# A short convolution and a SiLU feed-forward block: the output multiplication by 20 products over thirds and halves in place of 21, with nine sums made by DMAs that add

## Chip, cores and metric

The kernel runs on one core of one Trainium2 chip. The metric is the time of one execution on the device in microseconds; 2334.24 us is the median of three runs (2333.86 to 2334.28).

## What is computed

```python
# x (8, 4096, 192), weight (8, 7); w_in (192, 2048), w_out (2048, 192), all float32
w = softmax(weight, axis=-1)                       # one filter of 7 taps for each head of 24 channels
x_pad = concat([zeros((8, 6, 192)), x], axis=1)    # causal
out[b, s, h, g] = sum_k w[h, k] * x_pad[b, s + k, h, g]
x = out.reshape(32768, 192)
h = x @ w_in                                       # (32768, 2048)
g = h * (1 / (1 + exp(-h)))                        # SiLU
y = g @ w_out                                      # (32768, 192)
```

The weights arrive as float64 words and are rounded to float32 by integer operations at the start.

## The kernel before, in words

The 32768 tokens are worked in 32 blocks of 1024 (`TT`), each of two halves of 512 (`TB`). Block 0 is multiplied plainly (`up_plain`, `down_plain`) while the weights are still being prepared; blocks 1 to 31 use fast schemes that trade multiplications for additions.

Channels are worked in three thirds of 64 (`R`), and the 2048 hidden channels in 16 chunks of 128, in four groups of four (`NJ` = 4, index `j` or `g`).

**Up.** A block's hidden values `h` are made by 20 products (`PRODUCT`, `product`, L656) for each of the four groups. One product is a matmul with 64 rows of weights (half of TensorE's rows) that moves 512 columns, so two of them can run side by side. Their sums are finished by a list of small steps (`MICRO`, `micro`): copies and additions between PSUM banks (`b0` to `b6`), and into the tile `g`. `S13` to `S20` are the SiLUs on ScalarE, which leave eight slices `h0` to `h7` for each group in SBUF: four chunks of hidden channels, two token halves. Additions (`'a'`) are on VectorE; copies (`'c'`) are on ScalarE unless `ON_DVE` names them.

**Down, before.** `out_slot` (L746) works tiles of 32 output channels: six accumulators `acc0` to `acc5`, each fed for every group `j` and chunk `e` by four matmuls with 128 rows, 32 columns of weights and 512 moving columns, the four side by side in the columns of TensorE. For `acc5` the four move 128 columns each. Four of the operands are differences of slices of `g`, made by `sum_g` (L711), four for each group, each 128 partitions by 1024 elements, into a rotating tile `t`. The six accumulators are joined into `cmb` by `merge` (copies on ScalarE at L803, L808, L811; seven additions on VectorE at L823), turned by `turn_out` (L835) and stored by `store_out` (L845).

**Work beside it.** The next block's tokens are loaded (`load`, L289, on SP's queue), turned (`turn_in`, L548), convolved (`conv`: first tap on ScalarE at L579, six on VectorE at L582, for each third), spread over partitions by eleven SBUF to SBUF DMAs on SP's queue (`spread`, L599), and combined by six additions (`win`, L607). GpSimd does little after the start: one small copy a block (`halo_in`, L569).

**Order.** Every engine runs its instructions in program order, and that order is written out by hand: `START` for the first three blocks and `PLAN` for the steady state, strings of tokens such as `P7.0` (product 7 of group 0), `k8.2` (step k8 of group 2), `v.26` (third 2, tap 6), `sp.3`, `w.0`, `st.1`. A `+` marks the next block, a `-` the block before. So the next block's products follow the last output products of this one without a pause being written between them. PSUM has eight banks of 128 by 512, handed from step to step in the order in which they are freed (`at`, `TOUCHES`). `finish` is an ending of its own for the last block.

Of the kernel before, what the change touches and what calls it, by code (L numbers as in the profile page):

```python
# [9 lines left out]
F32 = mybir.dt.float32  # L10
I32 = mybir.dt.int32
# [6 lines left out]
def kernel(  # L18
# [40 lines left out]
    tpool = ctx.enter_context(tc.tile_pool(name="tp", bufs=3))  # L59
    gpool = ctx.enter_context(tc.tile_pool(name="gp", bufs=2 * NJ))  # L60
    upool = ctx.enter_context(tc.tile_pool(name="up", bufs=10))
# [28 lines left out]
    )  # L90
    START = (
# [1031 lines left out]
```

## Time and profile before

| | us |
|---|---|
| median of three runs | 2334.24 |
| the profiled execution, its own time | 2334.11 |
| its span, first to last instruction | 2332.4 |
| first fast product (L656) begins | 106.22 |
| one block in the steady state | 71.56 |
| last matmul ends | 2324.70 |

Mean granted TensorE clock 0.999. The busy shares are averages over the span; what a block costs is read from the chain of waits in order of time, which repeats itself with the block, and what each engine has left from the busy time in one block's window. Groups' busy times overlap each other on TensorE, where two or four matmuls run side by side, so its groups do not add up to the span. Every fp32 matmul shows as two records.

### The profile page before, as it was taken

To read this page: it belongs to the slowest core of one execution; us is meant where nothing else is said; L and a number is where in the kernel's file an instruction comes from. 1 tells how busy PE (TensorE), PEld (TensorE's weight loads), DVE (VectorE), ACT (ScalarE), POOL (GpSimd) and SP (SyncE) were. 2 spreads that over 40 slices of the span, in tenths; PEclk is the share of its full clock that TensorE was granted. 3 is DMA by queue.
4 is the path that set the end of the run, shared out by engine and by line. 5 is a ranking of instruction groups with operands and counts; after the bars stand their busy time and mean duration, and the time that the engine had idled before them with its cause. 6 is when DMAs were issued, how large, how long until landed. Compare 5 with 4: busy or idle time off the path is not lost.

```text
span 2332.4 us, 43764 instructions
## 1 busy us (share of the span) xinstructions
PE 2324.2 (100%) x17382; PEld 921.5 (40%) x17382; DVE 2178.5 (93%) x3045; ACT 1330.8 (57%) x2523; POOL 53.7 (2%) x84
## 2 busy tenths in 40 slices
PE   9999999999999999999999999999999999999998
PEld 5344343334333344333344333443334433334433
DVE  8999999999999999999999999999999999999996
ACT  5356655566654576545666555665457654566654
POOL 4200000000000000000000000000000000000000
PEclk9999999999999999999999999999999999999999
DMA  7211221212212222212122122221221221212211
GB/s 159 57 37 26 53 53 30 50 32 49 53 37 43 44 37 53 45 37 50 28 53 53 30 49 35 46 53 39 40 51 30 53 49 34 50 28 53 53 33 22
DMA packets 451246, 106.55 MB, mean 46 GB/s; under 512 B 423585, under 2 KB 428705, under 8 KB 451041
## 3 DMA queue, kind: packets, MB, share of 16 engines
q1 hardware_dynamic: 447392, 101.78, 23.3%
q8 instruction: 136, 2.23, 0.4%
q0 software_dynamic: 448, 1.58, 0.3%
q10 hardware_dynamic: 3200, 0.39, 0.1%
q14 instruction: 70, 0.57, 0.1%
HBM read 31.46 MB, written 25.17 MB: 24 GB/s over the span
## 4 chain that ended last, share of the span: by engine, by line
PE 95%; DVE 1%; SPq 0%; DMA 0%; issue 0%; ACT 0%; ACTq 0%
PE ps L746 48%; PE ps L656 47%; SPq L599 0%; DVE t L711 0%; DMA nat<-in_x_dram 0%; DVE win L607 0%; DVE u L678 0%; DVE w_other L257 0%; SPq L289 0%; DVE w_own L257 0%; DVE cmb L257 0%; DVE ps L694 0%; ACT u L257 0%; DVE g L694 0%; DVE wx L257 0%
## 5 line engine op out<-in xcount | busy, mean ns | idle before, releaser
L656 PE MATMUL ps<-win,w_own 64*128 64x512 f32 x1488 | 661.4, 598 | 0.8 <-DVE win L607 0.5
L746 PE MATMUL ps<-g,wo 128*32 128x512 f32 x2976 | 661.5, 592 | 0.0
L746 PE MATMUL ps<-t,wo 128*32 128x512 f32 (+1 forms) x4528 | 511.3, 447 | 0.0
L656 PE MATMUL ps<-dup,w_own 64*128 64x512 f32 x1240 | 492.5, 594 | 0.2 <-ACT ps L689 0.2
L746 PE MATMUL ps<-t,wx 128*32 128x512 f32 x2976 | 484.7, 592 | 0.0
L691 ACT ACTIVATE g<-ps 128x512 f32<-128x512 f32 x620 | 367.1, 599 | 186.6 <-DVE g L694 113.9
L656 PE MATMUL ps<-dup,w_other 64*128 64x512 f32 x1240 | 460.0, 595 | 0.0
L656 PE MATMUL ps<-win,w_other 64*128 64x512 f32 x992 | 444.6, 595 | 0.0
L694 DVE TENSOR_TENSOR g<-g,ps 128x512 f32<-128x512 f32 x496 | 331.3, 683 | 54.4 <-PE ps L656 35.4
L582 DVE SCALAR_TENSOR_TENSOR nat<-xt,turned,nat 128x512 f32<-128x512 f32 x558 | 378.2, 746 | 3.9 <-ACT nat L579 1.6
L808 ACT COPY yx<-ps 32x512 f32<-32x512 f32 x150 | 84.3, 579 | 516.7 <-PE ps L746 514.9
L656 PEld LDWEIGHTS ps<-win,w_own 64*128 64x128 f32 x1488 | 246.6, 186 | 211.4 <-issue 120.3
L711 DVE TENSOR_TENSOR t<-g,t 128x1024 f32<-128x1024 f32 x248 | 302.5, 1220 | 16.9 <-PE ps L746 9.6
L711 DVE TENSOR_TENSOR t<-g 128x1024 f32<-128x1024 f32 x248 | 300.6, 1212 | 13.3 <-PE ps L746 13.1
L746 PEld LDWEIGHTS ps<-t,wo 128*32 128x32 f32 x4528 | 175.1, 110 | 248.4 <-issue 189.9
L694 DVE TENSOR_TENSOR ps<-u,ps 128x512 f32<-128x512 f32 x372 | 255.3, 687 | 11.8 <-ACT u L687 5.2
L656 PEld LDWEIGHTS ps<-dup,w_own 64*128 64x128 f32 x1240 | 195.5, 186 | 142.7 <-issue 77.2
L746 PE MATMUL ps<-g,wx 128*32 128x512 f32 x1488 | 245.7, 592 | 0.0
L691 ACT ACTIVATE g<-g 128x512 f32<-128x512 f32 x372 | 220.8, 625 | 27.1 <-DVE g L694 23.6
L689 ACT ACTIVATE ps<-ps 128x512 f32<-128x512 f32 x372 | 214.5, 584 | 36.0 <-DVE ps L694 19.0
L746 PEld LDWEIGHTS ps<-g,wo 128*32 128x32 f32 x2976 | 173.1, 110 | 148.0 <-issue 147.2
L656 PEld LDWEIGHTS ps<-dup,w_other 64*128 64x128 f32 x1240 | 167.8, 186 | 131.3 <-ACT ps L689 50.3
(102 smaller groups left out, 1826.3 us busy)
## 6 DMA issues: line engine op xcount, KB each, us to landing
dup<-nat SPq DMA_DIRECT2D x221, 128.0 KB, 2.3
nat<-in_x_dram SPq DMA_DIRECT2D x382, 64.0 KB, 2.4
out_dram<-t SPq DMA_DIRECT2D x372, 64.0 KB, 2.0
win<-nat SPq DMA_DIRECT2D x124, 128.0 KB, 2.4
raw<-in_moe_w_out_dram SPq DMA_DIRECT2D x8, 384.0 KB, 3.9
raw<-in_moe_w_in_dram SPq DMA_DIRECT2D x12, 192.0 KB, 5.0
w_other<-w_own POOLq DMA_DIRECT2D x8, 192.0 KB, 5.6
raw<-in_moe_w_in_dram SPq DMA_DIRECT2D x6, 128.0 KB, 3.4
```

The source lines that it names most:

```text
L582: nc.vector.scalar_tensor_tensor(out=dst, in0=src, scalar=tap, in1=dst, op0=ALU.mult, op1=ALU.add)
L656: nc.tensor.matmul(at(b, "bank", to, g), raw(g, w, e), rows(slot_of(b, x_), e), start=first, stop=True, skip_group_check=True,)
L689: pin(nc.scalar.activation(seen[to], seen[u], AF.Copy, scale=-1.0))
L691: pin(nc.scalar.activation(seen[to], seen[u], AF.Silu, scale=float(sign)))
L694: pin(nc.vector.tensor_tensor(seen[to], seen[u], seen[v], op=op))
L711: pin(nc.vector.tensor_tensor(t[i // 2][:, i % 2, :], u, v, op=ALU.subtract))
L746: nc.tensor.matmul(acc[SQ * q : SQ * q + SQ, to], lhs[:, e, SQ * k : SQ * k + SQ], rhs[:, e, ts(q, TB // 4) if i == 5 else to], start=firs ...
L808: pin(nc.scalar.copy(to, acc(3 * (name[0] == "x") + k)[n:P, :]))
```

## The change

**Down, after.** The output is now made by 20 products (`OUT`) of 4 chunks by channel thirds by token halves. Groups are taken in pairs: `q` = 0 holds groups 0 and 1, `q` = 1 groups 2 and 3. One product `Qr.q` is four matmuls: for each of the pair's two groups (`e`) and each half `h` of the slot's 512 columns, one with 128 rows, 64 columns of weights and 256 moving columns, the two halves side by side in TensorE's columns.

```diff
+    def out_slot(b, r, q):
+        w, slot, name = OUT[r]
         acc = at(b, "bank", name)
+        for e in range(2):
+            for h in range(2):
+                pin(
+                    nc.tensor.matmul(
+                        acc[R * h : R * h + R, 0:HT],
+                        wd[:, 2 * q + e, w, :],
+                        g_all[:, q, slot, e, ts(h, HT)],
+                        start=False,
+                        stop=True,
+                        skip_group_check=True,
+                    )
+                )
```

**Operands.** All slices of `h` lie in one tile, `g_all`: two pairs, eleven slots (0 to 7 are the SiLUs' results, 8 to 10 are further), 128 by 1024 each. Thirteen sums for each pair work in place in it, 26 a block; nine of them are DMAs issued by GpSimd that add the source to the destination.

```diff
-        pin(nc.vector.tensor_tensor(t[i // 2][:, i % 2, :], u, v, op=ALU.subtract))
+    def sum_g(b, name, q):
+        sign, to, u, v = SUMS[name]
+        if f"{name}.{q}" in BY_DMA:
+            pin(
+                nc.gpsimd.dma_start(
+                    out=flat(g_all[:, q, to]), in_=flat(g_all[:, q, u + v - to]), accum_op=ALU.add
+                )
+            )
+            return
+        to, u, v = (flat(g_all[:, q, s]) for s in (to, u, v))
+        pin(nc.vector.tensor_tensor(to, u, v, op=ALU.add if sign > 0 else ALU.subtract))
...
+    SUMS = {'s1': (1, 8, 5, 3),
+            's2': (1, 9, 8, 2),
+            's4': (1, 7, 7, 5),
+            's3': (1, 9, 4, 9),
+            's6': (-1, 10, 0, 9),
+            's7': (1, 8, 8, 10),
+            's8': (1, 1, 1, 10),
+            's9': (1, 7, 7, 1),
+            's10': (-1, 5, 8, 7),
+            's12': (1, 5, 2, 5),
+            's0': (1, 3, 3, 2),
+            's5': (1, 6, 6, 4),
+            's11': (1, 6, 6, 7)}
...
+    BY_DMA = ('s0.0', 's0.1', 's11.0', 's11.1', 's4.0', 's4.1', 's7.0', 's7.1', 's8.1')
```

So `s8.1` is slot 1 plus slot 10 of pair 1. `OUT[r]` names the weights, the slot read and the bank; for this text: Q0, Q19, Q6 read slot 7 (as it came, after s4, after s9), Q13 and Q9 slot 8 (before and after s7), Q8 slot 10, Q16 slot 9, Q12 and Q10 slot 5 (after s10 and s12), Q5 slot 1, Q4 slot 6 after s11.

**Joining.** In place of `merge`: steps of the kind of `MICRO` on 128 by 256, of names with D: two zero fills on ScalarE and one on VectorE (`Dz`), twelve copies (`Dk`, `Dh`, `Du`; two on VectorE, ten on ScalarE), nine additions on VectorE (`Di`, `Dj`), and six transposes (`DS`) of 128 by 256 in place of four of 96 by 512. Stores are 2 times 4 DMAs of 96 KB a block in place of 4 times 3 of 64 KB. `finish` goes: the last block ends as every block does.

**Weights of the output.** `combine_out` makes the 20 combinations by 25 operations of 128 by 4 by 64 in four parts (`co.0` to `co.3`), which now stand among the first fast block's products, in place of 16 of 128 by 192, the first four of which stood ahead of them.

**Order.** `START` and `PLAN` are written anew. In the steady state the output products stand in this order, with VectorE's and GpSimd's steps between them (`*` marks the DMAs that add; P and the up steps left out):

```
s1.0 Q11.0 s2.0 v.05 s0.0* Q0.1 s4.1* Q11.1 Q13.0 s1.1 Q13.1 Q0.0 Q2.0 Q16.0 s2.1 Q16.1 Q19.1
s4.0* v.24 s3.0 Q14.0 Q14.1 s6.0 Q2.1 s7.0* Q8.0 s3.1 Q19.0 s6.1 v.16 Q1.1 Q8.1 s8.0 v.06 Q18.1
Q3.1 Q1.0 Q3.0 Q7.0 -DS13.0 s9.0 Q7.1 s10.0 Q12.0 Q18.0 sp.6 s8.1* sp.3 Q9.0 v.25 s9.1 s7.1* Q9.1
v.26 s5.1 -st.0 sp.0 s10.1 Q12.1 s12.0 Q10.0 +i.1 s12.1 Q6.0 Q6.1 Q10.1 Di12_7.0 s0.1* Q5.1 Q17.1
Q15.1 Q15.0 s5.0 Q17.0 s11.1* sp.5 +ld.2 +ld.0 +i.0 sp.7 sp.4 sp.8 Q5.0 sp.1 +i.2 sp.10 sp.9 s11.0*
w.0 sp.2 Q4.0 w.2 w.1 w.3 w.4 Q4.1 w.5 +P7.0 ...
```

`ON_DVE` names eleven copies of 128 by 512 in place of ten, besides the D steps above. Raw weights and the rounding's scratch lie in fixed places of `g_all`, `u_all` and `fin` in place of rotating tiles.

More of the change, by code (lines that the diff above doesn't have):

```diff
@@ L246 @@
     FLIPS = (1, 1, -1)
-    ON_DVE = ('h15.3', 'h18.0', 'k12.0', 'k12.1', 'k12.3', 'k8.0', 'u10.1', 'u10.2', 'u10.3', 'u6.2')
-    CLOSING = "S14.3"
+    ON_DVE = ('Dk15.0', 'Dk5.0', 'Dz1.0', 'h17.1', 'h17.3', 'h18.0', 'h18.3', 'k12.0', 'k12.1', 'k17.1',
+              'k8.3', 'k9.3', 'u10.0', 'u6.3')
+    SUMS = {'s1': (1, 8, 5, 3),
[11 more added lines that the diff above has]
+            's11': (1, 6, 6, 7)}
+    OUT = {0: (7, 7, 'ob0'),
+           1: (12, 6, 'ob1'),
+           2: (16, 5, 'ob8'),
+           3: (11, 6, 'ob3'),
+           4: (14, 6, 'ob5'),
+           5: (15, 1, 'ob7'),
+           6: (1, 7, 'ob0'),
+           7: (19, 0, 'ob3'),
+           8: (10, 10, 'ob3'),
+           9: (2, 8, 'ob4'),
+           10: (17, 5, 'ob2'),
+           11: (9, 1, 'ob0'),
+           12: (0, 5, 'ob0'),
+           13: (13, 8, 'ob1'),
+           14: (8, 2, 'ob6'),
+           15: (5, 9, 'ob3'),
+           16: (4, 9, 'ob1'),
+           17: (18, 3, 'ob2'),
+           18: (3, 4, 'ob1'),
+           19: (6, 7, 'ob8')}
+    COMBINE_OUT = [(1, 12, 10, 9), (-1, 13, 7, 8), (1, 14, 11, 9), (-1, 15, 6, 14), (-1, 16, 5, 8),
[4 rows of a table added]
+    NEGATE_OUT = [4, 19]
+    BY_DMA = ('s0.0', 's0.1', 's11.0', 's11.1', 's4.0', 's4.1', 's7.0', 's7.1', 's8.1')
+    SLOTS = 11
     def pin(ins):
@@ L276, in at, with flat @@
         return tile_
-    nats, xts, gs = {}, {}, {}
+    nats, xts = {}, {}
+    g_all = const.tile([P, 2, SLOTS, 2, TB], F32, name="g")
+    u_all = const.tile([P, 10, TB], F32, name="u")
+    HT = TB // 2
+    fin = const.tile([P, 14, HT], F32, name="fin")
+    def flat(t):
+        names = "abcd"[: len(t.shape) - 1]
+        return t.rearrange(f"p {' '.join(names)} -> p ({' '.join(names)})")
     def load(b, ks=range(NK)):
@@ L358 @@
     wr, ws = ([t[:, j] for j in range(NJ)] for t in (w_own, w_other))
-    wo = [const.tile([P, 2, 2, D], F32, name=f"wo{j}") for j in range(NJ)]
-    wx = [const.tile([P, 3, 2, HD], F32, name=f"wx{j}") for j in range(NJ)]
+    wd = const.tile([P, NJ, 20, R], F32, name="wd")
     raws = {}
     def raw_tile(key):
-        pool, tag = (gpool, "g") if key in (("i", 2), ("i", 3)) else (tpool, "t")
-        raws[key] = pool.tile([P, 4 * TB], I32, tag=tag, name="raw")[:, 0 : 2 * WC]
+        place = {
+            ("i", 0): g_all[:, 0, 8:10],
+            ("i", 1): g_all[:, 1, 8:10],
+            ("i", 2): fin[:, 0:6],
+            ("i", 3): fin[:, 6:12],
+            ("o", 0): u_all[:, 5:8],
+            ("o", 1): g_all[:, 0, 8:10],
+            ("o", 2): g_all[:, 1, 8:10],
+            ("o", 3): fin[:, 0:6],
+        }[key]
+        raws[key] = flat(place).bitcast(I32)[:, 0 : 2 * WC]
         return raws[key]
@@ L486, in combine, with combine_out @@
                 eng.tensor_scalar(both(to), both(u), scalar1=-1.0, scalar2=None, op0=ALU.mult)
-    def combine_out(j):
-        def a_(u, a):
-            return wo[j][:, a, :, HD * u : HD * u + HD]
-        x_ = [wx[j][:, i, :, :] for i in range(3)]
-        vec.tensor_tensor(x_[0], a_(1, 0), a_(1, 1), op=ALU.add)
-        vec.tensor_tensor(x_[1], x_[0], a_(0, 0), op=ALU.subtract)
-        vec.tensor_tensor(x_[2], a_(0, 1), x_[1], op=ALU.subtract)
-        vec.tensor_tensor(a_(1, 0), a_(0, 0), a_(1, 0), op=ALU.subtract)
+    def combine_out(part):
+        work = [*COMBINE_OUT, *((0, s, s, s) for s in NEGATE_OUT)]
+        n = (len(work) + 3) // 4
+        for sign, to, u, v in work[n * part : n * part + n]:
+            to, u, v = (wd[:, :, s, :] for s in (to, u, v))
+            if sign:
+                vec.tensor_tensor(to, u, v, op=ALU.add if sign > 0 else ALU.subtract)
+            else:
+                vec.tensor_scalar(to, u, scalar1=-1.0, scalar2=None, op0=ALU.mult)
     load_in(0, nc.sync, (0,))
@@ L616, in rows, with g_slot @@
         return t[R * e : R * e + R]
-    def g_tile(b, j, a):
-        if (b, j, a) not in gs:
-            gs[b, j, a] = gs[1, j, a] if b > 1 else gpool.tile([P, 2, 2, TB], F32, tag="g", name="g")
-        return gs[b, j, a]
+    def g_slot(j, c, n):
+        return g_all[:, j // 2, 2 * c + n, j % 2, :]
     def up_plain(b, j):
@@ L670, in place @@
             if x_[0] == "h":
-                c, n = divmod(int(x_[1:]), 2)
-                return g_tile(b, g, c // 2)[:, n, c % 2, :]
+                return g_slot(g, *divmod(int(x_[1:]), 2))
+            if x_[0] == "o":
+                if x_[1] == "b":
+                    return at(b, "bank", x_)[:, 0:HT]
+                return fin[:, (6 if x_[1] == "h" else 12) + int(x_[2:])]
             return at(b, "bank" if x_[0] == "b" else "up", x_, g)
-        seen = {x_: place(x_) for x_ in dict.fromkeys((to, u, v)) if x_}
+        seen = {x_: place(x_) for x_ in dict.fromkeys((to, u, v)) if isinstance(x_, str)}
         if kind == "c" and f"{name}.{g}" in ON_DVE:
@@ L689, in micro @@
                 pin(nc.scalar.activation(seen[to], seen[u], AF.Copy, scale=-1.0))
+        elif kind == "z":
+            if f"{name}.{g}" in ON_DVE:
+                pin(nc.vector.memset(seen[to], 0.0))
+            else:
+                to_ = seen[to].rearrange("p (x c) -> p x c", x=2)
+                pin(nc.scalar.copy(to_, zeros.unsqueeze(1).to_broadcast([P, 2, P])))
+        elif kind == "t":
+            k, n = to
+            pin(nc.vector.transpose(osb_all[:, NK * n + k, :], seen[u]))
         elif kind == "s":
@@ L713, in seed @@
-    def seed(b):
-        pin(nc.vector.memset(at(b, "bank", "acc5")[:, 0 : TB // 4], 0.0))
-    def out_slot(b, j, i, e, half=None):
-        w, x_ = wo[j], wx[j]
-        name = f"acc{6 if i == 3 and half else i}"
-        first = i != 5 and (b, name) not in begun
-        begun.add((b, name))
-        acc = at(b, "bank", name)
-        ts_ = {
-            k: held_at[b, f"t{k}", j] if half == 0 else sums_of(b, j, k)
-            for k in ((), (), (0,), (1,), (0, 1), (1,))[i]
-        }
-        def t(k):
-            return ts_[k // 2][:, k % 2, :].rearrange("p (e t) -> p e t", e=2)
-        a_ = [[w[:, a, :, HD * u : HD * u + HD] for a in range(2)] for u in range(2)]
-        forms = {
-            1: lambda: (a_[0][0], gs[b, j, 0][:, 0]),
-            2: lambda: (a_[0][1], gs[b, j, 1][:, 0]),
-            3: lambda: (x_[:, 2], gs[b, j, 1][:, 1]),
-            4: lambda: (a_[1][1], t(3)),
-            5: lambda: (x_[:, 0], t(0)),
-            6: lambda: (x_[:, 1], t(1)),
-            7: lambda: (a_[1][0], t(2)),
-        }
-        own, other, c = ((1, 2, 0), (3, 2, 1), (6, 2, 2), (7, 4, 0), (5, 4, 1), (4, 4, 2))[i]
-        for q in range(4):
-            lhs, rhs = forms[own if q < NP else other]()
-            k = c if i == 5 or q == NP else q
-            to = slice(0, TB // 4) if i == 5 else slice(0, TB) if half is None else ts(half, TB // 2)
-            pin(
-                nc.tensor.matmul(
-                    acc[SQ * q : SQ * q + SQ, to],
-                    lhs[:, e, SQ * k : SQ * k + SQ],
-                    rhs[:, e, ts(q, TB // 4) if i == 5 else to],
-                    start=first,
-                    stop=True,
-                    skip_group_check=True,
-                )
-            )
@@ L773, in down_plain @@
                             )
-                        if (a, e, k) == (1, 1, NK - 1):
-                            for c in range(2):
-                                del gs[b, j, c]
                         yield
     def copy_plain(b, k):
-        pin(nc.scalar.copy(cmbs[b][0][:, k, :], at(b, "bank", f"plain{k}")))
-    def merge(b, name, q):
-        n = HD
-        def acc(i):
-            return at(b, "bank", f"acc{i}")
-        if b not in cmbs:
-            new = b == 1
-            cmb = xpool.tile([P, 4, TB], F32, tag="cmb", name="cmb") if new else cmbs[1][0]
-            cmbs[b] = [cmb, {}]
-        cmb, t = cmbs[b]
-        c = [cmb[0:n, i, :] for i in range(4)]
-        if name[0] in "xy":
-            if name[0] not in t:
-                t[name[0]] = xpool.tile([P, TB], F32, tag="yx", name="yx", bufs=2)
-            k = int(name[1])
-            to = t[name[0]][SQ * k : SQ * k + SQ, :]
-            if name == "x2":
-                pin(
-                    nc.scalar.copy(
-                        to[:, ts(q, TB // 4)], acc(5)[SQ * q : SQ * q + SQ, 0 : TB // 4]
-                    )
-                )
-            else:
-                pin(nc.scalar.copy(to, acc(3 * (name[0] == "x") + k)[n:P, :]))
@@ new lines, in copy_plain, with turn_out, store_out @@
+        pin(nc.scalar.copy(plain[:, k, :], at(b, "bank", f"plain{k}")))
+    def turn_out(b, k):
+        pin(nc.vector.transpose(flat(osb_all[:, 2 * k : 2 * k + 2, :]), plain[:, k, :]))
+    def store_out(b, i):
+        if not b:
+            osb = osb_all.rearrange("p (k x) t -> p k (x t)", k=NK).rearrange(
+                "p k (a c) -> p k a c", c=SQ
+            )
+            for q in range(P // SQ):
+                c = R * i + SQ * (q % 2)
+                pin(
+                    nc.sync.dma_start(
+                        out=out_v[2 * b + q // 2][:, :, c : c + SQ],
+                        in_=osb[SQ * q : SQ * q + SQ, i, :, :],
+                    )
+                )
@@ L823, in merge @@
-        pin(nc.vector.tensor_tensor(out_, u, v, op=ALU.add))
-    osbs = {}
-    def osb_of(b):
-        t = at(b, "t", "osb" if b else "osb0")
-        return t.rearrange("p i (k c) -> p (i k c)", c=SQ).rearrange("p (i k c) -> p i k c", i=4, c=SQ)
-    def turn_out(b, i):
-        osb = osb_of(b)
-        top = HD if b else P
-        pin(
-            nc.vector.transpose(
-                osb[0:top, i, :, :].rearrange("p k c -> p (k c)"), cmbs[b][0][0:top, i, :]
-            )
-        )
-    def store_out(b, i):
-        osb = osb_of(b)
-        for q in range((HD if b else P) // SQ):
-            n, c = (i % 2, HD * (i // 2) + SQ * q) if b else (q // 2, R * i + SQ * (q % 2))
-            pin(
-                nc.sync.dma_start(
-                    out=out_v[2 * b + n][:, :, c : c + SQ],
-                    in_=osb[SQ * q : SQ * q + SQ, i, :, :],
-                )
-            )
+        osb = osb_all[:, NK * i : NK * i + NK, :].rearrange("p m (k c) -> p m k c", c=SQ)
@@ L851 @@
+        nk = HT // SQ
+        for r in range(P // SQ):
+            to = out_v[2 * b + i][:, nk * (r // 2) : nk * (r // 2) + nk, :]
+            to = to.rearrange("t k (m s c) -> t m k s c", m=NK, c=SQ)[:, :, :, r % 2, :]
+            pin(nc.sync.dma_start(out=to, in_=osb[SQ * r : SQ * r + SQ]))
     plan = [slot.split() for slot in (PLAN,)]
-    did, later = set(), []
+    did = set()
     BACK = {"-": 1, "=": 2, "+": -1}
     base = {t.lstrip("-=+") for s in plan for t in s}
-    held = {
-        t
-        for t in base
-        if t.split(".")[0] not in MICRO
-        and (t[0] in "Mzyxo" and t[:2] != "ze" or t[:2] == "st" or t[0] in "Dt" and int(t.split(".")[1][0]) >= NJ // 2)
-    }
@@ L867, in step @@
         if b < 0 or b >= NB or not name or (b, token) in did:
-            return
-        if b == NB - 1 and token in held:
-            return
-        if b == NB - 1 and token[:3] == "D3." and (b, CLOSING) not in did:
-            later.append(token)
             return
@@ L879, in step @@
             product(b, int(name[1:]), *digits)
-        elif name == "ze":
-            seed(b)
-        elif name == "t":
-            sum_g(b, *digits)
-        elif name[0] == "D":
-            i, (j, e) = int(name[1]), digits
-            for half in range(2) if i == 3 and b == NB - 1 else (None,):
-                out_slot(b, j, i, e, half)
-        elif name[0] in "Mzyx":
-            merge(b, name, *digits)
+        elif name[0] == "Q":
+            out_slot(b, int(name[1:]), *digits)
+        elif name in SUMS:
+            sum_g(b, name, *digits)
         elif name == "o":
@@ L1081 @@
     homes["bank"].extend(bank() for _ in range(8))
-    homes["up"].extend(upool.tile([P, TB], F32, tag="u", name="u") for _ in range(10))
-    homes["t"].extend(tpool.tile([P, 2, 2 * TB], F32, tag="t", name="t") for _ in range(3))
+    homes["up"].extend(u_all[:, i, :] for i in range(10))
     downs = down_plain(0)
```

180 lines of the change are left out of this document (53 added, 127 removed), and 186 rows, old and new, of tables (COMBINE_OUT, PLAN, START).

## The prediction, made before the changed kernel ran

> **What bounds the kernel now.** I read the page's first part, then the chain of waits, then one block of that chain in order of time, then what VectorE has left in that block.
>
> ```profile
> PE 2324.2 (100%) x17382; PEld 921.5 (40%) x17382; DVE 2178.5 (93%) x3045; ACT 1330.8 (57%) x2523; POOL 53.7 (2%) x84
> ...
> PE 95%; DVE 1%; SPq 0%; DMA 0%; issue 0%; ACT 0%; ACTq 0%
> ```
>
> TensorE is busy throughout and is 95% of the chain. A page's busy PE is not PE at its peak, so the chain's own steps decide (start us, length us, what):
>
> ```profile
> 749.59 33.29 PE ps L656 x151
> 782.88 1.85 PE ps L746 x16
> 784.73 1.92 PE ps L656 x8
> 786.65 34.50 PE ps L746 x368
> 821.15 33.29 PE ps L656 x151
> ```
>
> One block is 821.15 - 749.59 = 71.56 us: 33.29 + 1.92 = 35.21 of up products, 1.85 + 34.50 = 36.35 of output products. Neither part holds a wait. VectorE in the same 71.56 us (busy time of each engine in one window):
>
> ```profile
> 749.59:821.15 71.56, 71.56 (x546) 27.94 (x546) 67.09 (x93) 41.74 (x80) 0.11 (x1) 1.00 0.23 43
> ```
>
> 67.09 us of VectorE (67.4 is the mean of seven such blocks): the second limit stands only 4.2 us behind the first. So two questions decide: what TensorE's part shrinks by, and whether VectorE and the new DMAs still arrive in time.
>
> **TensorE.** Full output steps follow each other at 0.43 us (first and second record of the timeline's rows, four matmuls side by side):
>
> ```profile
> 789.62 0.60 PE L746 MATMUL ps<-t,wx 128*32 128x512 f32 x3
> ...
> 790.05 0.60 PE L746 MATMUL ps<-t,wx 128*32 128x512 f32 x3
> ```
>
> Before, a block has 80 such steps (five accumulators x 8 x 2 records) and 16 of 128 columns: 80 x 0.43 + 16 x 0.11 = 36.2, the 36.35 of the chain. After: 20 products x 2 pairs x 2 groups x 2 records = 160 steps of 256 columns, two matmuls of 128*64 side by side. Their price has two near rows, the last block's 256-column steps and block 0's 128*64 steps:
>
> ```profile
> L746 PE MATMUL ps<-t,wo 128*32 128x256 f32 x128 | 7.6, 379 | 0.0
> ...
> L765 PE MATMUL ps<-g,wo 128*64 128x512 f32 x192 | 41.6, 593 | 0.0
> ...
> L765 PEld LDWEIGHTS ps<-g,wo 128*64 128x64 f32 x192 | 13.6, 137 | 27.8 <-issue 27.2 <-ACT g L257 0.3 <-DVE nat L582 0.3
> ```
>
> The second gives 41.6 / 96 = 0.433 for 512 columns, 0.217 for 256. The first gives 7.6 / 32 = 0.24, which counts the overhang at the end of each run; its one run of 40 records begins 2304.44 and is 2.34 long, (2.34 - 0.38 + 0.217) / 10 = 0.217. The weight load, 137 ns, fits under 217. So 160 x 0.217 = 34.7 a block, bounds 34.7 and 38.4 (0.24). I take 34.7: 36.35 - 34.7 = 1.65 us saved a block, 31 blocks: -51.2 us. The up part stays at 35.21, and a block at 69.9.
>
> **VectorE**, by busy time over count in its rows. Removed a block: 16 sums of 1.216 (302.5 + 300.6 over 496) = 19.5; seven merge additions (101.7 + 40.5 over 30 blocks) = 4.7; four transposes 2.8; a fill 0.2: 27.2. Added: 17 sums on VectorE (26 less nine) x 1.216 = 20.7; nine additions of 256 columns at 0.39 (the last block's 96x256 row) = 3.5; six transposes of 256 at 0.43 = 2.6; one copy 0.68; two narrow copies and a fill 0.9: 28.4. Net +1.2, so 67.4 + 1.2 = 68.6 of 69.9. This fits with 1.3 us over, where 4.2 were: no cost while nothing else is late, and a wait on VectorE of more than about 1.3 us a block reaches TensorE. ScalarE gains ten narrow copies and loses ten merge copies, at 41.7 of 69.9: nothing.
>
> **The adding DMAs.** No row shows one. Nearest is the only bulk transfer on GpSimd's queue:
>
> ```profile
> w_other<-w_own POOLq DMA_DIRECT2D x8, 192.0 KB, 5.6
> ...
> DMA to landing us min/median/max: 3.2/5.6/6.7
> ...
> q0 software_dynamic: 448, 1.58, 0.3%
> ```
>
> Its data moved at 1.58 MB in 0.3% x 2332.4 = 7.0 us, 226 GB/s, so 192 KB take 0.9 and the fixed part is 3.2 - 0.9 = 2.3; issued in pairs (1.7 us of data) 5.6 - 1.7 = 3.9. An adding DMA moves 512 KB: 2.3 us of data if the second operand costs nothing, 4.6 if it is read as a second transfer. Bounds of issue to landing: 2.3 + 2.3 = 4.6 and 3.9 + 4.6 = 8.5. I take 6.0: the lower fixed part, since DMA engines were seven tenths busy when those rows ran and are at 0.23 in a block, and data midway. GpSimd itself has nothing else (0.11 us in the block; an issue 0.5 to 0.9), and no DMA waits behind an unready one for long, as they stand in the order in which they come ready.
>
> By the Trainium skill ("DMA: Bandwidth & Descriptors", "Anatomy of one DMA - SWDGE (gpsimd) path") such a DMA takes about 2.0 us and its bytes over 436 GB/s, an estimate of 3.2 us for 512 KB. The 192 KB row took 3.2 at the least where this gives 2.4; by it none would be late, and the sum below would lose its stall.
>
> Time that the order leaves, each by what stands between (TensorE 0.87 for a Q, 4 x 0.217; VectorE 1.216 a sum, 0.68 a tap): s4.1, issued after Q0.1, is needed by Q19.1: seven Q, 6.1 us. s4.0 to Q19.0: eight, 7.0. s7.0, issued after s6.0, to s10.0: four sums, two taps, a transpose, 6.6. s8.1 after s6.1 to s9.1: three sums, three taps, a transpose, 6.1. s7.1 to s10.1: 9.2. s11.0 after s5.0 to Q4.0: 25 Q from Q8.0 to Q4.0 are 21.75, VectorE's steps from s6.0's end to s5.0's end 17.6 (11 sums, four taps, a transpose, an i, a D), so 4.2 and VectorE's lead at s6.0, at least 0.85 by Q16.1, which needs s2.1: 5.0. At 6.0 all but the last are just in time; s11.0 may be late by up to 1.0, and Q4.0 holds up TensorE's queue, the next block's P7.0 behind it. Behind a late s10 or s9 stand VectorE's taps and `w`, for which P7.0 and P1.0 wait. I take 0.3 us a block, 9 us.
>
> SP's queue: between sp.3 and the last sp stand four stores and eight loads at 0.5 each (rows of 12 loads: 6.36 us), then seven spreads at 0.6; sp.9 is issued about 12 us after v.06 and lands 2.3 later, when VectorE, some 14 us of steps on, comes to w.0. Up to 0.7 late, inside the 1.3.
>
> **Start and end.** `co` is 25 operations of 256 columns at 0.42 (the w_own rows) = 10.5 in place of 5.8, most of it in block 1, where VectorE is now full: +3 (bounds 0 and 8). At the end, after Q4.1: two additions and six transposes on VectorE, 3.0, but SP's eight stores at 0.55 end by 6.3, and land 2.0 to 2.5 later: 8.6 after the last matmul, against 2332.4 - 2324.7 = 7.7: +1.
>
> **Sum** against the span 2332.4: -51.2 + 9 + 3 + 1 = 2294.2; the run's own time stood 1.7 above its span and is the median within 0.2: **2296 us**. Its own range, 2278 (no stall, no cost at the start) to 2308.
>
> **Rivals.**
> (A) The adding DMAs land late, and TensorE waits in each block. Its place is Q19.1, Q4.0 and, through s9.1 and s10.0, VectorE. One wait gives the others lead, so the largest lateness counts: landing less 5.0. It decides from 1.65 us, a landing of 6.7: slower beyond. If the second operand is a second read, 2.3 + 4.6 = 6.9: 1.9 a block, +0.25 x 31 + 4: 2346. At 8.5: 3.5 a block, 2395. For: nine transfers a block where none were, and six of them within 20 us. Against: the DMA share of 0.23.
>
> The Trainium skill ("Collectives: The Full Stack", "The bandwidth ceiling") says that an add in a DMA is slow because it needs two source reads, which halves the rate; that is this rival, and no run here shows it yet.
>
> (B) VectorE becomes the bound: it keeps half of its 4.2 us of waiting for TensorE and ScalarE, 68.6 + 2.1 = 70.7 a block: -0.86 x 31 + 4 + 1.7, 2311. For: 98% filled, and in the rows VectorE waits for ps and g in every block. Against: those waits are where it was ahead.
> (C) The change doesn't save TensorE time, because narrow steps take 0.24: 38.4 a block, +2.05 x 31 + 4 + 1.7: 2402. Against: the rows of 0.217 in both forms.
>
> **Chances.** Forecast 0.47, A 0.30, B 0.15, C 0.03, and 0.05 for no change. 0.2% (4.7 us) is about what a measurement of this kernel can tell. Faster: forecast and B, 0.62; slower: most of A, and C, 0.32; within: the rest, with A's beginning, 0.06. Range: 2274, a little below the forecast's own since the up part's 35.21 may shrink to its 80 x 0.43 = 34.4 in some blocks, to 2362, which leaves A's upper half and C out.
>
> **What would show it.** Right: a block of about 70.2 in the chain, output steps of 0.217, landings near 6 us on GpSimd's queue, VectorE at 98%. A shows as TensorE's weight loads idle at Q19.1 or Q4.0, or VectorE at s9 and s10, released by a DMA g<-g, and landings over 6.7. B shows a chain that runs through VectorE with no DMA. C shows steps of 0.24 or more. Wrong altogether: a block above 71.56 with landings under 6.

## The result and the profile after

The changed kernel takes 2726.49 us (median of four runs, 2722.55 to 2730.28) where the kernel before takes 2334.05 on the same chip: 1.168 times as long (95% interval 1.166 to 1.170). The prediction was 2296, in a range of 2274 to 2362. The profiled execution has a span of 2726.1 us, 393.7 more than before.

From the page of the changed kernel (busy times, DMA queues, DMA issues):

```profile
PE 2438.6 (89%) x15334; PEld 1473.7 (54%) x15334; DVE 2210.1 (81%) x3296; ACT 1308.4 (48%) x2553; POOL 286.3 (11%) x363
...
PEclk9999988999898999889989889889899888999999
...
q0 software_dynamic: 40624, 147.87, 29.6%
...
g<-g POOLq DMA_DIRECT2D x279, 512.0 KB, 6.0
...
out_dram<-fin SPq DMA_DIRECT2D x248, 96.0 KB, 3.2
win<-nat SPq DMA_DIRECT2D x124, 128.0 KB, 5.0
```

No engine is full any more: TensorE fell from 100% to 89% of the span, VectorE from 93% to 81%. The adding DMAs land (from issue until the data has arrived) after 6.0 us in the median, the figure that the prediction took. `PEclk` now has eights in it: the granted clock of TensorE drops again and again. And transfers that the change did not touch have become slow: the spreads `win<-nat` land after 5.0 us where they took 2.4. The other seven spreads of a block, `dup<-nat`, keep their median of 2.3; what delays them is shown below.

The waits of VectorE and TensorE in the same run (what waited, for what: us in total, times, longest):

```profile
DVE xt L623 <- DMA nat<-in_x_dram: 290.4, 27, 12.2
...
PE ps L799 <- DVE ps L779: 195.0, 28, 8.5
...
DVE dup L682 <- DMA dup<-nat: 63.6, 26, 8.7
...
DVE g L791 <- DMA g<-g: 45.7, 59, 2.7
```

The largest wait has nothing to do with the adds' results. In 27 of 31 blocks VectorE waits some 10.8 us for the loads of the next block's x (L623 is `i`, the transposes of the loaded rows). VectorE's waits for the adds themselves (L791, the sums) are 1.5 us a block; TensorE's, in the same view, are 10.8 us in the whole run (L799, 13 times).

One block in order of time. First SP's queue, start us, length us, transfers (issues side by side make one row):

```profile
1425.85 2.28 SPq L674 DMA_DIRECT2D win<-nat  x2
1428.19 11.31 SPq L853 DMA_DIRECT2D out_dram<-fin  x4
1439.54 1.85 SPq L674 DMA_DIRECT2D dup<-nat  x1
1441.44 1.17 SPq L674 DMA_DIRECT2D win<-nat  x1
1442.65 6.40 SPq L357 DMA_DIRECT2D nat<-in_x_dram  x8
1449.15 3.68 SPq L674 DMA_DIRECT2D dup<-nat  x6
...
1455.29 2.72 SPq L853 DMA_DIRECT2D out_dram<-fin  x4
```

The four stores of `st.0` hold SP for 11.31 us, 2.83 each. The four of `st.1`, 27 us later and of the same form, take 2.72 together, 0.68 each. What differs is what GpSimd's queue has just issued (the same view of GpSimd):

```profile
1418.24 0.85 POOL L785 DMA_DIRECT2D g<-g  x1 [2.37 <-PE ps L799]
1423.03 0.85 POOL L785 DMA_DIRECT2D g<-g  x1 [3.94 <-DVE g L791]
1425.42 2.60 POOL L785 DMA_DIRECT2D g<-g  x3 [1.54 <-DVE g L791]
```

Five adds of 512 KB within 10 us. Behind them stand, in SP's order, first the stores, then the loads. VectorE and TensorE at that time (the bracket is the idle time before the row and what ended it):

```profile
1451.02 1.31 DVE L623 STREAM_TRANSPOSE xt<-nat 128x512 f32<-128x512 f32 x2 [9.79 <-DMA nat<-in_x_dram]
1452.25 0.40 DVE L779 TENSOR_TENSOR ps<-fin,ps 128x256 f32<-128x256 f32 x1
1454.74 2.01 DVE L682 TENSOR_TENSOR dup<-dup 128x512 f32<-128x512 f32 x3 [2.09 <-DMA dup<-nat]
```

```profile
1452.71 3.68 PE L799 MATMUL ps<-g,wd 128*64 128x256 f32 x16 [6.09 <-DVE ps L779]
1458.23 2.04 PE L729 MATMUL ps<-win,w_own 64*128 64x512 f32 x2 [1.84 <-DVE win L682]
```

VectorE executes in order. It stands 9.79 us at `i.0`; the merge addition `Dj9.0` of 0.40 us stands behind it, and TensorE's `Q4.0` needs that merge. So a load for the next block holds the output of this one. Then the spreads are 2.09 late for `w.0`. TensorE's clock and the DMA engines in steps of 5 us (the busy times of PE, PEld, DVE, ACT, POOL; granted clock; DMA share; GB/s):

```profile
1440.00:1445.00 5.00, 5.00 (x50) 3.33 (x48) 1.23 (x2) 0.82 (x3) 0.85 (x1) 1.00 1.03 193
1445.00:1450.00 5.00, 1.62 (x16) 0.80 (x12) 0.00 (x0) 0.86 (x3) 0.00 (x0) 1.00 0.83 143
1450.00:1455.00 5.00, 2.29 (x12) 1.34 (x14) 1.89 (x4) 0.00 (x0) 0.00 (x0) 0.68 0.85 193
1455.00:1460.00 5.00, 3.16 (x11) 1.37 (x9) 4.93 (x11) 1.95 (x3) 0.00 (x0) 0.50 0.57 93
```

The DMA share is 1.03: the engines are full. And after TensorE's pause its clock is halved, for 10 to 14 us in 27 of the 31 blocks, 362 us in the whole run (4.5 before).

From one `i.0` to the next this block is 85.15 us (1451.02 to 1536.17); from first product to first product the median block is 85.1, where 69.9 were forecast. VectorE is busy for 68.3 of the 85.15. It waits 10.3 for the loads (ahead of the second `i.0`), 2.6 for adds and 2.1 for the spreads; the rest is small gaps.

### The profile page after: what moved, and what is told of

Same layout as the page of the kernel before. It is cut to its first block, busy times and chain, and to the rows that moved or that the text cites. A ratio compares the mean times of both kernels' runs of the same rounds, so it can differ in the third digit from the quotient of the medians.

```text
span 2726.1 us, 40825 instructions
## 1 busy us (share of the span) xinstructions
PE 2438.6 (89%) x15334; PEld 1473.7 (54%) x15334; DVE 2210.1 (81%) x3296; ACT 1308.4 (48%) x2553; POOL 286.3 (11%) x363
## 3 DMA queue, kind: packets, MB, share of 16 engines
q0 software_dynamic: 40624, 147.87, 29.6%
## 5 line engine op out<-in xcount | busy, mean ns | idle before, releaser
L799 PE MATMUL ps<-g,wd 128*64 128x256 f32 x9920 | 1159.1, 393 | 214.2 <-DVE ps L779 195.0
L799 PEld LDWEIGHTS ps<-g,wd 128*64 128x64 f32 x9920 | 714.8, 141 | 667.7 <-DVE ps L779 207.7
L791 DVE TENSOR_TENSOR g<-g 128x1024 f32<-128x1024 f32 x527 | 634.8, 1216 | 52.8 <-DMA g<-g 45.7
L729 PE MATMUL ps<-win,w_other 64*128 64x512 f32 x992 | 501.3, 673 | 0.5
L785 POOL DMA_DIRECT2D g<-g x279 | 239.0, 960 | 2302.4 <-PE ps L729 909.0
L623 DVE STREAM_TRANSPOSE xt<-nat 128x512 f32<-128x512 f32 x96 | 64.5, 696 | 290.6 <-DMA nat<-in_x_dram 290.4
L779 DVE TENSOR_TENSOR ps<-u,ps 128x512 f32<-128x512 f32 x372 | 253.6, 689 | 16.9 <-ACT ps L765 12.3
L729 PEld LDWEIGHTS ps<-dup,w_own 64*128 64x128 f32 x1240 | 209.7, 186 | 103.4 <-issue 27.7
L729 PEld LDWEIGHTS ps<-win,w_other 64*128 64x128 f32 x992 | 194.8, 212 | 113.4 <-issue 58.4
L729 PEld LDWEIGHTS ps<-dup,w_other 64*128 64x128 f32 x1240 | 205.7, 186 | 88.3 <-issue 26.2
L654 ACT ACTIVATE nat<-xt,turned 128x512 f32<-128x512 f32 x93 | 60.6, 712 | 316.2 <-DMA xt<-xt 229.3
L763 ACT COPY u<-ps 128x512 f32<-128x512 f32 x310 | 176.6, 592 | 48.3 <-PE ps L729 44.2
L765 ACT ACTIVATE fin<-ps 128x256 f32<-128x256 f32 x93 | 35.6, 383 | 256.8 <-PE ps L799 256.8
```

What stands on the lines that cost most here:

```text
L623: nc.vector.transpose(xts[b][:, k, pad : pad + TB], nats[b][:, k, :, :].rearrange("p k c -> p (k c)"))
L654: pin(nc.scalar.activation(dst, src, AF.Copy, scale=tap))
L729: nc.tensor.matmul(at(b, "bank", to, g), raw(g, w, e), rows(slot_of(b, x_), e), start=first, stop=True, skip_group_check=True,)
L763: pin(nc.scalar.copy(seen[to], seen[u]))
L765: pin(nc.scalar.activation(seen[to], seen[u], AF.Copy, scale=-1.0))
L779: pin(nc.vector.tensor_tensor(seen[to], seen[u], seen[v], op=op))
```

## Experiments

Three causes are in the trace, and they are tangled. **T**: the order in SP's queue, with the loads behind stores whose issue takes 11 us. **R1**: the adding transfers fill the DMA engines, so whatever is moved, the next transfer beside them is late. **R2**: the halved clock, as a cause of its own. All edits are made in the changed kernel, most of them in its `PLAN` (the fragments show neighbouring tokens). A token that was already done for a block is skipped at its later place. A time without a range is that of a single run, and a block's length is a median.

**The stores later (e1_st).** `st.0` moves some 40 us, into the next block's products.

```diff
-DS14.0 +j10.0
+DS14.0 st.0 +j10.0
```

> Only the four stores of the first half (st.0) move: from the middle of the output products, where four adding DMAs are in flight, to the products of the next block, where none is. Theory T: SP's queue runs in order, the stores take 11.3 us to issue while the adds hold the DMA engines, and the eight loads behind them land too late for VectorE's i.0 (9.8 us of waiting a block). Then i.0's wait falls below 4 us, and the time to 2500 us or less. Rival R1: the DMA engines are short in that stretch whatever stands first, so the loads meet the same adds: wait stays above 7 us, time above 2650. Rival R2: the halved clock is its own cause and not a result of TensorE's idle time: the half-speed stretches (10 to 14 us a block) stay though the wait is shorter.

Measured: 2590.18 us, block 79.6, and `i.0` still waits 162.5 us in 27 blocks (6 each). That lies between the two forecasts.

**The loads earlier (e2_ld).** All three loads of a block stand together, ahead of the adds.

```diff
-+ld.1 S16.1
++ld.1 +ld.2 +ld.0 S16.1
-Dh14.0 +ld.2 +ld.0 +i.0
+Dh14.0 +i.0
```

> Only the eight loads ld.2 and ld.0 move, from behind the stores to behind ld.1, some 40 us earlier. T: i.0 no longer waits at all; the spreads are still behind the slow stores, so w.0 waits 2 to 5 us; TensorE idles 2 to 4 us; a block of 72 to 76, time 2330 to 2460. R1 says the same of the loads, but w.0 waits as long as i.0 did: above 2550. R2: half-speed stretches stay, above 2500.

Measured: 2618.48, block 80.7. The wait at `i.0` is gone, and the spreads have taken its place:

```profile
DVE dup L682 <- DMA dup<-nat: 248.4, 29, 9.8
```

These are R1's numbers, but T's order is in them too: the stores of `st.0` still block SP (12.12 us for four), and now it is the spreads behind them that are late.

**Both (e3_both)**, the two edits together.

> Stores and loads both move. T: SP's queue is empty when the spreads come, nothing waits for it; TensorE idles under 1.5 us a block, the clock stays granted in full, a block of 70 to 71.5, time 2290 to 2340. R1: the spreads alone still land late beside the adds, w.0 waits over 5 us, above 2400. R2: half-speed stretches stay, above 2450.

Measured: 2453.76 us (2450.17 to 2456.31), 1.051 of the kernel before (1.049 to 1.053); block 74.8. So 273 of the 392 us come back by the order in SP's queue alone. But T's own 2290 to 2340 was missed: the spreads still wait, and six of them hold SP for 9.05 us, 1.5 each:

```profile
DVE dup L682 <- DMA dup<-nat: 103.4, 24, 8.5
```

```profile
1452.31 9.05 SPq L674 DMA_DIRECT2D dup<-nat  x6
```

T has most of it, R1 the rest. The halved time went with TensorE's pauses: 362 us in the changed kernel, 190 in e1_st and in e2_ld, 46 here. So the halved clock follows the pauses, and R2 falls; what it costs is the next question.

**The clock (e4_warm).** Ten matmuls of zeros, added into a bank of sums, fill TensorE's pause before `Q4.0`.

> The changed kernel with ten matmuls of zeros (128 x 256, adding nothing, into a bank that Q5 has filled) between Q5.0 and Q4.0, where TensorE has its 6 us pause. T: i.0's wait stays at 9 to 10 us, but TensorE is not idle and the half-speed stretches shrink or go; each costs 5 to 7 us, so the block falls from 85.3 to 78 to 81, time 2490 to 2600. R2: half-speed stretches stay as long as they were, time 2700 to 2750.

Measured: 2742.36 us, block 85.5. The halved time did fall, from 362 to 252 us, and nothing was gained. In this stretch VectorE is the limit: in the 5 us where the changed kernel's clock is 0.50, VectorE is busy for 4.93. The Trainium skill ("TensorE: Matmul & The Clock Gate", "HAM oscillation — how this bites in real kernels") prices such a stretch at half its length. By that, as an estimate, the 110 us less would have given 55 us; the trace shows nothing of it, as the slow matmuls lie beside VectorE's work. What this run can't exclude is a cost of the ten matmuls that hid a smaller gain.

**No adds at all (e5_noadd).** All 26 sums on VectorE, loads and stores where the change has them.

```diff
-    BY_DMA = ('s0.0', 's0.1', 's11.0', 's11.1', 's4.0', 's4.1', 's7.0', 's7.1', 's8.1')
+    BY_DMA = ()
```

> The changed kernel with all 26 sums on VectorE, no adding DMA; stores and loads stay where the change puts them (no +ld or st token is moved). Theory (adding transfers fill the DMA engines and so stretch SP's issues and delay the spreads): SP's issues return to 0.5-0.6 us each although they stand in the same order, i.0 no longer waits 10 us (under 1.5), w.0 under 1.5, the clock is not halved; the block is VectorE's 68.3 + 9 x 1.216 = 79.3 and about 1 of small waits, 80 against 85.3: about 2560 us, faster than the changed kernel though VectorE does 11 us more a block. Rival (the order alone is too late, loads behind stores and the output transposes): i.0 still waits over 4 us beside the 79.3: over 2650.

Measured: 2584.81 us, faster than the changed kernel with 10 us more of VectorE's sums in each block (960.3 us in the run in place of 634.8). The block is 79.2, and VectorE sets it: it is busy for 97% of the span. SP's queue in it, same order as above:

```profile
1445.94 3.74 SPq L853 DMA_DIRECT2D out_dram<-fin  x4
1449.73 0.65 SPq L674 DMA_DIRECT2D dup<-nat  x1
1450.42 0.59 SPq L674 DMA_DIRECT2D win<-nat  x1
1451.06 4.37 SPq L357 DMA_DIRECT2D nat<-in_x_dram  x8
1455.53 3.67 SPq L674 DMA_DIRECT2D dup<-nat  x6
```

Stores 0.94 each in place of 2.83, loads 0.55 in place of 0.80. From the first store to the last load's issue it takes 9.5 us instead of 20.9. VectorE waits for neither loads nor spreads. This settles what stretched SP's queue: the adds in flight. In this block the order alone costs nothing; whether it would in one of 70 us, where the loads have less time, no run shows. So it took both, the adds and the order: e3_both returns most of the loss with the adds kept, and e5_noadd returns the issue times with the order kept.

**One add out of the crowd (e6_s01, e7_s01_s11v, e9_s01b).** In e3_both five of the nine adds are issued in the last 20 us before the next block, beside the spreads. The first try moved `s0.1` behind `s1.1`.

> e3_both with one adding DMA, s0.1, issued some 10 us earlier (behind s1.1), out of the last 20 us of the block where the DMA share is 1.03. Theory (bytes of the DMA engines in that stretch): 512 KB less in it are 2.9 us, so w.0's wait falls from 5.3 to 2-3 us and the block from 74.8 to about 72: 2360 to 2390. Rival (the spreads are late because VectorE makes their input late, or SP issues them one after another at its own price): no change, 2440 to 2460.

> e6_s01 with s11.1 on VectorE instead of a DMA: eight adding DMAs a block, two fewer than e3_both in the last 20 us. Theory: w.0's wait gone (under 1), VectorE 68.0 + 1.2 = 69.2 busy and about 1.5 of small waits, block 70.5 to 71.5: 2300 to 2335, ratio to the kernel before 0.985 to 1.0. Rival (SP's own issue price): w.0 still waits about 5, block over 75.

Measured: 2612.55, and 2616.24 (1.121 of before, 1.119 to 1.123). In that place `s0.1` takes slot 2 before its last writes, so another sum is computed, and ScalarE, which makes those writes, has to wait for the DMA. From the waits of e6_s01:

```profile
ACT g L776 <- DMA g<-g: 220.3, 29, 8.7
```

They say nothing of the theory. Placed behind `s4.0`, where both operands are final:

```diff
-Dk5.0 s4.0 v.24
+Dk5.0 s4.0 s0.1 v.24
-Dk13.0 s0.1 Q5.1
+Dk13.0 Q5.1
```

> e3_both with the adding DMA s0.1 issued behind s4.0, some 7 us earlier than in e3_both and behind s2.1, so that both its operands are final (in e6_s01 it stood before ScalarE's last writes of slot 2). Theory (bytes of the DMA engines in the last 20 us of the block): w.0's wait falls from 5.3 to 2-3 us, block 72 to 73: 2370 to 2410. Rival (SP's own issue price, or VectorE's late input): 2440 to 2460.

Measured: 2413.57, block 73.4. The spreads' wait fell from 103.4 us to 10.9, more than forecast; the block fell less, as waits for adds on VectorE rose from 41.7 to 86.9 us, and on TensorE from 41.1 to 49.9:

```profile
DVE g L791 <- DMA g<-g: 86.9, 76, 2.4
...
PE ps L799 <- DMA g<-g: 49.9, 39, 3.3
```

One transfer of 512 KB, issued 8 us earlier, is worth 40 us of the run. What is left is of rival A's kind: adds that land late for sums and for products.

**The spreads on another queue (e8_actq).** Six of the eleven on ScalarE's, on top of e3_both.

```diff
-        pin(nc.sync.dma_start(out=rows(slot_of(b, s), e), in_=rows(src, half)))
+        queue = nc.scalar if b and n in (1, 2, 4, 8, 9, 10) else nc.sync
+        pin(queue.dma_start(out=rows(slot_of(b, s), e), in_=rows(src, half)))
```

> e3_both with six of the eleven spreads (1, 2, 4, 8, 9, 10) issued on ScalarE's queue instead of SP's. Theory (DMA engines full): the spreads' data wait for the engines whichever queue issues them; w.0's wait stays 4-6 us, block 74-76, 2430 to 2480 (more if ScalarE is held in its issues). Rival (SP issues one after another, 1.5 us each): two queues issue side by side, w.0's wait falls by 4 us or more, 2330 to 2370.

Measured: 2610.17, outside both forecasts, and inconclusive: in ScalarE's order the issues stand behind copies that wait for TensorE, and go out late for that reason (at 1471.20, just after a copy that had waited 3.07 us for a matmul). It tells nothing of the DMA engines.

**Fewer adds (e10_s01_s11v, e11_two_v).** `s11.1` back on VectorE, on top of e9_s01b; and `s0.1` and `s11.1` back on VectorE, on top of e3_both.

> e9_s01b with s11.1 on VectorE instead of a DMA: two adding DMAs fewer than e3_both in the last 20 us. Theory: w.0's wait under 1 us, VectorE 69.2 busy and 1.5 of small waits, block 70.5 to 71.5: 2310 to 2345, ratio to the kernel before 0.99 to 1.005. Rival (SP's issue price): w.0 still waits 4 or more, block over 74, over 2430.

> e3_both with s0.1 and s11.1 on VectorE, at their places: seven adding DMAs. Theory: w.0's wait under 1 us as in e10_s01_s11v, but VectorE 70.4 busy and 1.5 of small waits, block 71.7 to 72.5: 2345 to 2375. Rival (SP's issue price): w.0 waits 4 or more, over 2440.

Measured: 2408.76 (1.032 of before, 1.030 to 1.033), block 73.6; and 2413.45, block 73.6. The spreads' wait is gone in both, as the theory had it, but the block stays where e9_s01b had it, and both times missed their forecasts. Some 3.7 us a block above the 69.9 of TensorE's work were left.

**Is it VectorE's amount of work? (e12_s7v, e13_act).** `s7.1`, the add that landed last in e10_s01_s11v (10.6 us), goes to VectorE, on top of e9_s01b; then three narrow operations go from VectorE to ScalarE.

```diff
-    BY_DMA = ('s0.0', 's0.1', 's11.0', 's11.1', 's4.0', 's4.1', 's7.0', 's7.1', 's8.1')
+    BY_DMA = ('s0.0', 's0.1', 's11.0', 's11.1', 's4.0', 's4.1', 's7.0', 's8.1')
-    ON_DVE = ('Dk15.0', 'Dk5.0', 'Dz1.0', 'h17.1', 'h17.3', 'h18.0', 'h18.3', 'k12.0', 'k12.1', 'k17.1',
+    ON_DVE = ('h17.1', 'h17.3', 'h18.0', 'h18.3', 'k12.0', 'k12.1', 'k17.1',
```

> e9_s01b with s7.1 on VectorE instead of a DMA (in e10_s01_s11v it was the adding DMA that landed last: issued behind s8.1 in one pair, 10.0 us to landing, and both s10.1 on VectorE and Q9.1 on TensorE waited 1.4 to 1.6 for it). Theory (what is left over e10's 69.0 of VectorE work is waiting for adds that land late in a crowd): VectorE 69.2 busy, waits down from 4.0 to 1.5-2, block 70.7 to 71.3: 2315 to 2345. Rival (VectorE needs some 3.5 to 4 us of slack whatever is taken away, as in e11_two_v): block 73 to 73.5, 2395 to 2410.

> e12_s7v with three narrow operations of the output part (Dk15.0, Dk5.0, Dz1.0: two copies and a fill of 128x256, 1.1 us together) on ScalarE instead of VectorE. If VectorE sets the block: another 1 us a block, 69.8 to 70.5, 2285 to 2315, faster than the kernel before. If TensorE or an add's landing sets it: no change against e12_s7v (within 8 us).

Measured: 2419.57 (1.037; 1.035 to 1.038) and 2418.89 (1.037; 1.035 to 1.038). Taking 1.1 us of work off VectorE changed nothing, so its amount was not what held the block. Nor did s7.1 leaving the queue help, as `s8.1` was late in its place (7.3 us from issue to landing in the median, where the prediction had left it 6.1). VectorE in e12_s7v, in order of time:

```profile
1579.09 2.36 DVE L791 TENSOR_TENSOR g<-g 128x1024 f32<-128x1024 f32 x2 [1.48 <-DMA g<-g]
```

This is `s9.1`, waiting 1.48 us for `s8.1`, and `s7.1` behind it; `s10.1` behind it then comes too late for TensorE:

```profile
1584.43 13.13 PE L799 MATMUL ps<-g,wd 128*64 128x256 f32 x104 [1.85 <-DVE g L791]
```

**The waiter later (e14_s9late, e16_s9only, e15_s8v).** Nothing is taken out; `s9.1` moves 3 us later in VectorE's order, on top of e13_act and of e12_s7v. In e15_s8v `s8.1` goes to VectorE too.

```diff
-v.25 s9.1 Dh17.0 s7.1 Q9.1 v.26 s5.1 -st.0
+v.25 Dh17.0 s7.1 Q9.1 v.26 s5.1 s9.1 -st.0
```

> e13_act with the sum s9.1, which waits for the adding DMA s8.1, moved 3 us later in VectorE's order, behind s7.1, a tap and s5.1. In e13_act VectorE waits 1.5 to 2.2 a block for s8.1, and s10.1 behind it then holds Q12.1 on TensorE 1.5 to 1.85. Theory (what is left is this one landing): both waits go, block 71 to 72, 2340 to 2365. Rival (an add that is late shows up at the next place, as s7.1 and s8.1 did after the spreads): block 73 to 73.6, 2400 to 2420.

> e14_s9late with s8.1 on VectorE too: seven adding DMAs, VectorE 69.2 busy. Theory: no add stands beside the spreads any more; waits of VectorE about 1, block 70.2 to 71.2, 2315 to 2345. Rival: the last add s11.0 (Q4.0 waits 0.7 to 1.4 for it in e10 and e11) or VectorE's sum holds it at 72 to 73.5, 2365 to 2410.

> e14_s9late without ScalarE's three narrow operations (Dk15.0, Dk5.0, Dz1.0 are back on VectorE, 69.2 busy): s9.1's move alone on top of e12_s7v. Theory (the landing of s8.1 is what held it, the amount of VectorE's work is not): the block falls by the same 1.7-1.9 us as from e13_act to e14_s9late, to 71.7-72.2, 2355 to 2380. Rival (with the late add gone VectorE's amount decides): 72.5 to 73.2, 2385 to 2405.

Measured: e14_s9late 2365.93 (1.014; 1.013 to 1.016), e16_s9only 2364.28 (1.013; 1.011 to 1.015), e15_s8v 2399.93 (1.029; 1.027 to 1.030). The move alone is worth 55 us (2419.57 to 2364.28), with or without the three operations on ScalarE: the last 2 us a block were the landing of `s8.1`, which still takes 7.3 us here; only its reader stands later. The waits of e16_s9only, against 45.7 and 63.6 in the changed kernel (the loads' 290.4 are 0.3):

```profile
DVE g L791 <- DMA g<-g: 8.9, 17, 1.4
...
DVE dup L682 <- DMA dup<-nat: 5.8, 4, 2.1
```

e15_s8v went against the theory: with that sum on VectorE too, `s10.1` comes late to TensorE again, for VectorE's own work this time (TensorE waits 35.3 us in 31 blocks for such a sum, 13.4 in e16_s9only). So here, and not in e13_act, the amount counts.

No version beats the kernel before. e16_s9only has a median block of 71.7, as before (71.56). Its profiled execution is 26.6 us longer: 17 until block 2 starts, 6 in blocks somewhat longer on average (71.90 against 71.68), and 3 in the last block and the end. Its output part is as long as before: from one matmul's start to the next, a median block spends 35.6 us in up products and 36.1 in output products, where the kernel before has 35.2 and 36.35. So the 1.65 us a block that the 20 products should have saved show in no run.

## Why the prediction was wrong

**TensorE: the step right, the part not reached.** Four records of an output step's form follow each other at 0.432 us in the median, 0.216 a step of two where 0.217 was taken. Rival C (steps of 0.24) fell. But the part of 34.7 us asks that every step follows at once. The best version has 36.1: 0.7 of the difference is `Q12.1`, late behind `s10.1`, 0.2 `Q10.0`, and about one step in twenty takes 0.27. The up part is 0.4 longer too, now that `Q11.0` stands among its products.

**VectorE: right in amount.** 68.3 us busy in the block where 68.6 were worked out. It is not what set the block in the changed kernel, so rival B fell as the cause; e5_noadd and e15_s8v show where it would begin to decide.

**The adds' landing: the median right by luck.** 6.0 was taken and 6.0 measured, but no single size is behind it. By place in the block the medians are 4.5 us for the four adds that stand apart (`s0.0`, `s4.1`, `s4.0`, `s7.0`), 6.0, 9.3 and 12.3 for the three issued together (`s8.1`, `s7.1`, `s0.1`), 9.1 for `s11.1` and 7.1 for `s11.0`. The prediction took one landing for all nine, and did not ask what they do to each other. Rival A had the right sign, and its signs are there: VectorE waits 45.7 us for adds and TensorE 10.8, together a seventh of the loss. Once SP's queue was in order (e9_s01b, 80 us above the kernel before), more time for the reader of one late add returned 49 of these (e16_s9only). What made most of the loss in the changed kernel was the adds' effect on other transfers, and neither the forecast nor A has that.

**SP's queue: the step that failed.** The prediction counted "four stores and eight loads at 0.5 each", then "seven spreads at 0.6", and found them "up to 0.7 late, inside the 1.3". The stores and loads were counted right. The durations were taken from rows of the kernel before, where no bulk transfer ran beside them. Beside five adds the four stores took 11.31 and the eight loads 6.40, where the step had 6.0 for all twelve; the two spreads that stand between them took 3.0 more. It also asked only who waits for the spreads. The loads had a reader too, `i.0`, and behind it in VectorE's order stood a merge that the current block's last output product needs. The loads then cost VectorE 290.4 us in the run and, behind it, TensorE 195.0, where the prediction had nothing. e1 to e3 return 273 us by moving these transfers, e5 returns the issue times without moving them.

**The DMA share.** Against A the prediction set "the DMA share of 0.23". That is a mean over the block. Nine adds at 2.86 us of full engines each (147.87 MB in 29.6% of 2726.1 us are 183 GB/s) are 25.7 us, and they are issued within 33 us of the block (1408.90 to 1441.43; the last packet ends at 1446.74), beside the first four spreads, half the stores and the start of the eight loads. In the last 20 us of that stretch (1425 to 1445) the share is 0.97 to 1.05.

**The halved clock: not foreseen, and no cost that was found** (e4_warm).

**The start: mis-sized.** `co` in block 1 was priced at +3 (bounds 0 and 8). Block 2 starts at 196.96 us where it was 175.60, and at 192.50 in e16_s9only: +17. Of the 21.4 us, 3.5 are there when block 1's first product begins (104.50 us, and 100.98 before; the 106.22 of the table is a later row of the chain). In block 1 VectorE is busy for 80.5 us where it was 71.7 (windows from block 1's first product to block 2's), and TensorE waits 7.7 us for `win`, behind spreads that come 5.7 late, and 4.4 for a merge. So SP's queue has a share in this too; how the rest divides no run shows, as no experiment changed the order of the first blocks.

**The end: also short.** The table's 2324.70 is where the chain leaves TensorE; the last matmul of the kernel before ends at 2326.36, 6.0 us before the end of the span. In the changed kernel it is 10.0 us, so the end costs 4 us and not 1.

**Two small sums.** The prediction's own terms without a stall and without a cost at the start give 2284, not 2278, and its parts of a landing, 2.3 us and 3.45 of data, give 5.8, not 6.0. Neither bears on the miss.

**The sum.** 21.4 us until block 2; then 29 blocks of 84.3 in place of 71.7 are 367; the last block and the end 5: the 393.7.

## What to carry to other kernels

Price a DMA issue by the traffic that will be in flight when it runs, stretch by stretch, and not by rows of a quieter kernel: here bulk transfers on a queue that had been idle made another queue's issues up to three times as long. For each transfer that stands behind such an issue, name its reader, and what stands behind that reader on an in-order engine, be it of another block. When a stall is removed and another appears, look for the one transfer that lands last; here moving its reader behind 3 us of work that was there anyway gave 55 us, and taking 1.1 us of work a block away gave nothing.

## What the hardware showed that was not expected

- An adding DMA within the core's memory of 512 KB moved at 183 GB/s and landed after 4.5, 6.0 and 13.2 us (min, median, max). The Trainium skill's rule for such a DMA ("DMA: Bandwidth & Descriptors", "Anatomy of one DMA - SWDGE (gpsimd) path"), from which the prediction estimated 3.2 us, is too low here even for the fastest. The Trainium skill also says, of reductions between cores, that a second source read halves the rate ("Collectives: The Full Stack", "The bandwidth ceiling"). The trace fits that here: an add's fastest packet took 0.327 us for 4096 bytes, 12.5 GB/s on one of the 16 engines. The fastest packet of the plain copies on the same queue, before, took 0.233 us for 6144, 26 GB/s. The 226 GB/s that the prediction took for the plain copies is a mean beside other traffic; no such copy ran alone on that queue, so this is not settled.
- SP's own issue instruction takes longer while adds are in flight: in the changed kernel 114 of 260 stores take 1.4 us or more, up to 6.3. Without adds, in the same order (e5_noadd), it is one of 260. The spreads `dup<-nat` take 1.6 us of SP's time in the median in e3_both, and 0.6 in e5_noadd.
- The Trainium skill says that each DMA engine takes turns between the queues, a packet at a time ("DMA: Bandwidth & Descriptors", "Queues, rings and completion order"). The spreads agree with that: the 128 KB of `dup<-nat` landed after 2.3 us in e5_noadd and after 6.4 beside the adds in e3_both, slowed without being stopped.
